# Stage 1 of a three-block kernel: small PSUM transposes in quarters of one bank, up-projections on the general ring

## The chip, the cores and the metric

One NeuronCore of one Trainium2 chip runs the whole program. The metric is device time in microseconds (us), the median of repeated runs; lower is better. The engines are PE (TensorE: matmuls and transposes), ACT (ScalarE), DVE (VectorE), POOL (GpSimd) and SP, which here only issues DMAs. Each engine takes its own instructions strictly in order, and waits at an instruction until the semaphores that it names have been raised. PSUM, where PE writes its results, has eight banks of 128 partitions by 512 fp32 values.

## The reference

Three blocks follow each other on a batch of 8 sequences of 576 tokens and 512 features; only the first, with the token half of the second, matters for the change.

```python
a = exp(phi - max(phi, axis=seq)); a = a / sum(a, axis=seq)      # phi: 8, 8 heads, 576, 32
k_m, v_m = einsum('bhsm,bhsd->bhmd', a, k), einsum('bhsm,bhsd->bhmd', a, v)
attn = softmax(q @ k_m.T / sqrt(64)); x = attn @ v_m             # 576 x 64 per head
u = x + (relu(x.T @ w_tok1) @ w_tok2).T                          # mixes tokens
x = u + relu(u @ w_ch1) @ w_ch2                                  # mixes channels: up, then down
# then a mixture of 4 causal attention experts, two for each token
```

## The kernel before

Most matrix products are made of three: each fp32 operand is split in a high part (fp32r) and the rest, and hi·hi, hi·lo and lo·hi are summed in PSUM (`mm3`, whose matmuls all have line 250). Scores, transposes and the sums over the sequence run in plain fp32 on PE.

Stage 1 goes over 16 units: one batch row and four heads each. A unit has three parts. `front` takes the maximum of phi over the sequence (DVE `top`, then PE transposes it, `top_t`; DVE reduces, `top_c`; PE transposes the result back over all partitions, `top_b`; DVE subtracts, `e_sub`; ACT takes exp), sums k and v with it on PE (`kv_mm`, tile g), scales k (DVE `k_scale`, tile kr; ACT, tile ks), transposes k (`k_t`, copied out by ACT `k_c`, tile kmT) and transposes q (`q_t`: two full banks of four transposes each, and a small one of the last 32 rows, copied to qTb). `rows` makes the scores, their softmax and the transposes of the attention (`to_rows`, a full bank; `to_rows_end`, a small one read by ACT `hi5` and DVE `lo5`). `mix` does the token product and writes u (`u_a`, `u_b`). At the end `ahead` reloads the first 512 columns of u and computes the first four up-projections of the next stage (`up`, 12 matmuls each, whose results go through ACT `up_hi` and DVE `up_lo`). Stage 2 goes on with the down-projections, tiles o0 to o3.

The order on every engine in stage 1 is not written out by hand. A planner (`Plan`) holds each step with an assumed length, its inputs and the PSUM ring that it takes a place of; `search` shuffles the steps' ranks 400 times, keeps the order that ends first by its own reckoning, and so writes all five queues. A change in the rings therefore reorders the whole stage. `filled` puts idle matmuls (`spin`, 128 by 128 zeros in bf16) in the gaps that the planner sees on PE in its first 70 us. The waits themselves are set later by the framework, from what each instruction reads and writes.

In stage 1 the eight banks of PSUM are: ring t with two banks (all transposes, large and small, one to a bank), ring g with four (everything else), and two banks h of a pool `ppw` of their own, that hold the first up-projections and the target of the spins. `ppw` lives on into stage 2.

Of the kernel before, what the change touches and what calls it, by code (L numbers as in the profile page):

```python
# [10 lines left out]
F32 = mybir.dt.float32  # L11
# [4 lines left out]
AF = mybir.ActivationFunctionType  # L16
OP = mybir.AluOpType
AX = mybir.AxisListType
PSUM = bass.MemoryType.PSUM
# [190 lines left out]
def fused_kernel(ctx: ExitStack, tc, q, k, v, phi, w_tok1, w_tok2, w_ch1, w_ch2,  # L210
# [3 lines left out]
    M = phi.shape[3]  # L214
# [7 lines left out]
    SH = S // 2  # L222
# [4 lines left out]
    PE, ACT, DVE, POOL, SP = nc.tensor, nc.scalar, nc.vector, nc.gpsimd, nc.sync  # L227
# [62 lines left out]
    wch_ctx, b0_ctx, stg_ctx, sw_ctx = ExitStack(), ExitStack(), ExitStack(), ExitStack()  # L290
    wbm = wch_ctx.enter_context(tc.tile_pool(name="wbm", bufs=1, reuse_waits="tile"))
    wu = b0_ctx.enter_context(tc.tile_pool(name="wu", bufs=1, reuse_waits="tile", side="right"))
    ppw = sw_ctx.enter_context(tc.tile_pool(name="ppw", bufs=1, space=PSUM, reuse_waits="tile", side="right"))
    w1h, w1l, w2h, w2l = {}, {}, {}, {}

    def ch_weights(pool, spool, fc, wd, nb, ws=(0, 1)):
# [21 lines left out]
    with ExitStack() as sa:  # L318
# [24 lines left out]
        for i in range(NB2):  # L343
# [2 lines left out]
        units = [(b, g) for b in range(B) for g in range(2)]  # L346
        NU, NR = len(units), 2
        NB = S // 32
        plan = Plan(pools=dict(t=2, g=4, h=2, cst=5, cy=2, cm=2),
                    ahead=dict(PE=0, ACT=90, DVE=70, POOL=-60),  # L350
                    hop=dict(PE=230, ACT=60, DVE=120, POOL=120, SP=1900), stay=2000)
        add, free = plan.add, plan.free
        MM, TR = 133.4, 109

        def psum(name, shape=(128, 512)):
            return pp.tile(list(shape), F32, name=name, bufs=4 if name == "g" else 2)

        def loads(n):
            b, g = units[n]
# [25 lines left out]
        def front(n):  # L385
# [7 lines left out]
                DVE.tensor_reduce(mx[:], ph[:].rearrange("p h j m -> p h m j"), axis=AX.X, op=OP.max)  # L393

            def top_t():
                st["p"] = psum("t", (128, 128))
                PE.transpose(st["p"][:], st["mx"][:].rearrange("p h m -> p (h m)"), ident[:])

            def top_c():
                st["mc"] = wk_.tile([128, 1], F32, name="pmc", bufs=2)  # L400
                DVE.tensor_reduce(st["mc"][:], st["p"][:], axis=AX.X, op=OP.max)

            def top_b():
                st["p"] = psum("t", (128, 128))
                PE.transpose(st["p"][:], st["mc"][:].to_broadcast([128, 128]), ident[:])

            def e_sub():
                e = st["e"] = wk_.tile([128, 4, 5, M], F32, name="ea", bufs=2)
                bc = st["p"][:].rearrange("p (h m) -> p h m", h=4)[:, :, None, :].to_broadcast([128, 4, 5, M])
                DVE.tensor_sub(e[:], ph[:], bc)  # L410

            def e_exp():
# [51 lines left out]
                POOL.tensor_mul(st[y][:], src[:, None, :].to_broadcast([128, 4, 64]), vmask[:])  # L464

            def k_t():
                st["p"] = psum("t", (128, 128))
                PE.transpose(st["p"][:], st["ks"][:].rearrange("p a d -> p (a d)"), ident[:])

            def k_c():  # L470
                st["km"] = wk_.tile([128, 128], F32, name="kmT", bufs=2)
                ACT.activation(st["km"][:], st["p"][:], AF.Copy)

            def q_t(i):
                if i < 2:
                    p = st["q", i] = psum("t")
                    for x in range(4):
                        PE.transpose(p[:, 128 * x:128 * x + 128],  # L478
                                     qn_[:, 2 * i + x // 2, 2 * (x % 2):2 * (x % 2) + 2, :].rearrange("p j d -> p (j d)"),
                                     ident[:])  # L480
                    return
                st["q", 2] = psum("t", (128, 4, 32))
                for h in range(4):
                    PE.transpose(st["q", 2][:, h, :], qe_[:, h, :], ident[0:32, 0:32])

            def q_c(i):
                if i < 2:
                    ACT.activation(qT[:, 2 * i:2 * i + 2, 0:256].rearrange("k h (p j) -> k h j p", j=2),
                                   st["q", i][:].rearrange("k (h j p) -> k h j p", h=2, j=2), AF.Copy)
                else:  # L490
                    ACT.activation(qT[:, :, 256:SH], st["q", 2][:], AF.Copy)

            add("DVE", 1320, top, reads=[kph], writes=["mx"])
            a = add("PE", TR, top_t, kind="f", reads=["mx"], writes=[(n, "pt")], take="t")
            c = add("DVE", 270, top_c, reads=[(n, "pt")], writes=[(n, "mc")])
            free(a, c)
            a = add("PE", TR, top_b, kind="f", reads=[(n, "mc")], writes=[(n, "pb")], take="t")
            c = add("DVE", 820, e_sub, reads=[(n, "pb"), kph], writes=[("e", n % 2)])
            free(a, c)
            add("ACT", 735, e_exp, reads=[("e", n % 2)], writes=[("e", n % 2)])  # L500
# [6 lines left out]
            c = add("ACT", 360, k_mul, reads=[(n, "g"), (n, "r")], writes=["ks"])  # L507
            d = add("ACT", 315, v_scale, reads=[(n, "g"), (n, "r")], writes=["vm"])
            free(g_, c, d)
            a = add("PE", TR, k_t, kind="f", reads=["ks"], writes=[(n, "pk")], take="t")  # L510
            c = add("ACT", 260, k_c, reads=[(n, "pk")], writes=[kkm])
            free(a, c)
            add("POOL", 560, v_split, reads=["vm"], writes=["vh", "vl"], port=True)
            add("POOL", 760, lambda: v_mask("vh", "Vh"), reads=["vh"], writes=[("Vh", n % 3)], port=True)
            add("POOL", 760, lambda: v_mask("vl", "Vl"), reads=["vl"], writes=[("Vl", n % 3)], port=True)
            for i in range(3):
                a = add("PE", (440, 440, 400)[i], lambda i=i: q_t(i), kind="f", reads=["qn"], writes=[(n, "q", i)], take="t")
                c = add("ACT", (625, 625, 275)[i], lambda i=i: q_c(i), reads=[(n, "q", i)], writes=[(*kqT, i)])
                free(a, c)

        def rows(n):
# [44 lines left out]
                    PE.transpose(p[:, 128 * j:128 * j + 128], st["a"][:, 128 * j:128 * j + 128], ident[:])  # L566

            def to_rows_end():
                st["p5"] = psum("t", (128, 128))
                PE.transpose(st["p5"][0:ST, :], st["a"][:, SM:S], ident[:])  # L570

            def hi4():
# [30 lines left out]
            h4 = add("ACT", 600, hi4, reads=[(n, "p4")], writes=["hi4"])  # L603
            l4 = add("DVE", 690, lo4, reads=[(n, "p4"), "hi4"], writes=["lo4"])
            free(a4, h4, l4)
            a5 = add("PE", TR, to_rows_end, kind="f", reads=[("a", n % 2)], writes=[(n, "p5")], take="t")
            h5 = add("ACT", 265, hi5, reads=[(n, "p5"), "hi4"], writes=["hi5"])
            l5 = add("DVE", 285, lo5, reads=[(n, "p5"), "hi5"], writes=["lo5"])
            free(a5, h5, l5)
# [94 lines left out]
        def ahead():  # L704
            def opened():
                stg_ctx.close()
                ld_ctx.close()
                st["b0"] = b0_ctx.enter_context(tc.tile_pool(name="b0", bufs=1, reuse_waits="tile", side="right"))
                load_u(0, st["b0"])
                uh[0] = st["b0"].tile([128, KD, 512], F32R, name="uh")  # L710
                ul[0] = st["b0"].tile([128, KD, 512], F32R, name="ul")

            def s_hi(kd):
                ACT.activation(uh[0][:, kd, :], ub[0][:, kd, :], AF.Copy)

            def s_lo(kd):
                DVE.tensor_sub(ul[0][:, kd, :], ub[0][:, kd, :], f(uh[0][:, kd, :]))

            def up(fc):
                st[fc] = ppw.tile([128, 512], F32, name="h", bufs=2)  # L720
                mm3(st[fc][:], [((w1h[fc][:, kd, :], w1l[fc][:, kd, :]), (uh[0][:, kd, :], ul[0][:, kd, :]))
                                for kd in range(KD)])

            def up_hi(fc):
                hs[0, fc] = [st["b0"].tile([128, 512], F32R, name=x, bufs=4) for x in ("hh", "hl")]
                ACT.activation(hs[0, fc][0][:], st[fc][:], AF.Relu)

            def up_lo(fc):
                DVE.scalar_tensor_tensor(hs[0, fc][1][:], st[fc][:], 0.0, f(hs[0, fc][0][:]), op0=OP.max, op1=OP.subtract)

            st = rest
            add("SP", (600, 4300), opened, reads=[("ud", 0), ("ud", 1)], writes=["ub"], after=[U[NU - 1]["score"], *convs])
            for kd in range(KD):
                add("ACT", 600, lambda kd=kd: s_hi(kd), reads=["ub"], writes=[("bh", kd)])
                add("DVE", 700, lambda kd=kd: s_lo(kd), reads=["ub", ("bh", kd)], writes=[("bl", kd)], port=True)
            for fc in range(NA):
                a = add("PE", 12 * 227, lambda fc=fc: up(fc), reads=[(x, kd) for x in ("bh", "bl") for kd in range(KD)] + [("w1", fc)],
                        writes=[("up", fc)], take="h")
                c = add("ACT", 600, lambda fc=fc: up_hi(fc), reads=[("up", fc)], writes=[("fh", fc)])
                d = add("DVE", 690, lambda fc=fc: up_lo(fc), reads=[("up", fc), ("fh", fc)], writes=[("fl", fc)])  # L740
                free(a, c, d)
# [112 lines left out]
        ahead()  # L854
        ET = mybir.EngineType
        with tc.manual_schedule(engines={ET.PE, ET.Activation, ET.DVE, ET.Pool, ET.SP}):
            idle = ppw.tile([128, 512], F32, name="h", bufs=2)

            def spin():
                PE.matmul(idle[:, 0:128], lhsT=still[:, 0:128], rhs=still[:], start=True, stop=True)  # L860

            for fn in plan.filled(70000, 0.6, 56, spin):
                fn()
# [35 lines left out]
    with ExitStack() as sb:  # L899
# [3 lines left out]
        wkx = wkx_ctx.enter_context(tc.tile_pool(name="wkx", bufs=1, reuse_waits="tile"))  # L903
        stg = stg_ctx.enter_context(tc.tile_pool(name="stgb", bufs=2, reuse_waits="tile"))
        pp = sb.enter_context(tc.tile_pool(name="ppb", bufs=1, space=PSUM, reuse_waits="tile"))
        def split_pool(n):
            return wkx if n % 2 else wk_

# [756 lines left out]
```

## Time and profile before

| | |
|---|---|
| median of 3 runs | 1188.08 us (1187.22 to 1189.03) |
| profiled execution | 1188.45 us, of which the trace's span is 1186.7 us |
| PE busy | 1162.8 us (98% of the span) |
| DVE, ACT, POOL busy | 785.3, 594.2, 406.6 us |
| granted TensorE clock, mean | 0.997 |

Busy time of PE contains the spins, and a matmul's end is modelled, so that a busy PE may still be short of its peak. The first matmul of stage 2's down-projections stands at 241.7 us: stage 1 is the first fifth of the span.

### The profile page before, as it was taken

The page shows a single profiled execution, that of the slowest core. Times are in us where ns is not written, and L with a number is a line of the kernel's source. Part 1 is how long each engine was busy: PE and PEld are TensorE (multiplying, and loading weights), DVE is VectorE, ACT ScalarE, POOL GpSimd, SP SyncE. Part 2 cuts the span into 40 slices and gives each one's busy share as a digit, 9 for nine tenths or more (in the row PEclk, how much of TensorE's full clock was granted, in tenths as well). Part 3 has the DMA queues.
Part 4 walks back from the last instruction along what each step waited for, and adds up shares of the span by engine and source line. Part 5 has one row for each costly group of instructions (what it writes and reads, how often), then busy time and mean ns, then how long its engine had stood idle before and what let it go on. Part 6 is the DMA issues. An engine that isn't in the chain of part 4 may idle for free.

```text
span 1186.7 us, 23501 instructions
## 1 busy us (share of the span) xinstructions
PE 1162.8 (98%) x8668; PEld 1055.3 (89%) x8668; DVE 785.3 (66%) x1942; ACT 594.2 (50%) x1533; POOL 406.6 (34%) x575
## 2 busy tenths in 40 slices
PE   7999999999999999999999999999999999999998
PEld 6778878888888999898998889999999999999986
DVE  6889997386755656647563624877766777677763
ACT  3566666443322222313221214777676767676774
POOL 3667566100001010101000445637272727373331
PEclk9999999999999999999999999999999999999999
DMA  9888884262030312203020444313232323222423
GB/s 274 224 256 254 264 263 162 73 218 66 17 107 1 107 36 72 81 27 107 1 99 1 146 134 121 103 46 104 66 114 65 122 84 109 79 83 62 160 88 107
DMA packets 125075, 133.54 MB, mean 113 GB/s; under 512 B 35232, under 2 KB 94624, under 8 KB 124960
## 3 DMA queue, kind: packets, MB, share of 16 engines
q1 hardware_dynamic: 124960, 132.03, 37.1%
q8 instruction: 69, 1.13, 0.4%
q14 instruction: 46, 0.38, 0.1%
HBM read 89.01 MB, written 31.46 MB: 102 GB/s over the span
## 4 chain that ended last, share of the span: by engine, by line
PE 84%; DVE 8%; POOL 2%; issue 2%; ACT 2%; DMA 1%; SPq 0%; ACTq 0%; DVEq 0%; POOLq 0%
PE g L250 23%; PE o L250 21%; PE h L250 20%; PE y L1437 4%; PE s L1328 3%; PE t L1392 3%; PE s L1350 1%; PE g L662 1%; PE g L668 1%; PE g L671 1%; PE g L669 1%; POOL a L1373 1%; PE t L478 1%; PE t L250 1%; DVE pmx L393 1%
## 5 line engine op out<-in xcount | busy, mean ns | idle before, releaser
L978 POOL TENSOR_TENSOR tl<-ub,th 128x512 fp32r<-128x512 f32 x12 | 18.2, 1539 | 358.4 <-ACT th L977 358.4
L250 PE MATMUL o<-hl,w2h 128*128 128x512 f32 x360 | 141.0, 392 | 0.0
L250 PE MATMUL o<-hh,w2l 128*128 128x512 f32 x360 | 140.6, 391 | 0.0
L250 PE MATMUL o<-hh,w2h 128*128 128x512 f32 x360 | 135.5, 391 | 0.0
L1373 POOL TENSOR_TENSOR a<-a,cf 128x128 f32<-128x128 f32 (+3 forms) x128 | 88.3, 724 | 70.6 <-DVE cf L1365 63.6
L930 ACT ACTIVATE hh<-m 128x256 fp32r<-128x256 f32 x120 | 48.9, 417 | 126.0 <-DVE m L1001 65.9
L1317 DVE CUSTOM_DVE_ANT_0 ssb<-s,cmask 128x128 f32<-128x128 f32 (+2 forms) x144 | 68.8, 483 | 31.1 <-PE s L1328 18.2
L250 PE MATMUL h<-uh,w1l 128*128 128x512 f32 (+2 forms) x248 | 82.6, 335 | 0.0
L250 PE MATMUL h<-uh,w1h 128*128 128x512 f32 (+2 forms) x248 | 82.6, 334 | 0.0
L250 PE MATMUL h<-ul,w1h 128*128 128x512 f32 (+2 forms) x248 | 82.4, 335 | 0.0
L1330 ACT ACTIVATE a<-ssb,nb 128x128 f32<-128x128 f32 (+3 forms) x128 | 71.4, 558 | 21.3 <-DVE nb L1317 17.7
L250 PEld LDWEIGHTS o<-hh,w2l 128*128 128x128 f32 x360 | 67.6, 188 | 14.4
L250 PEld LDWEIGHTS o<-hl,w2h 128*128 128x128 f32 x360 | 67.6, 188 | 12.6 <-DVE hl L923 0.5
L250 PEld LDWEIGHTS o<-hh,w2h 128*128 128x128 f32 x360 | 67.6, 188 | 12.3
L931 DVE SCALAR_TENSOR_TENSOR hl<-m,hh 128x256 fp32r<-128x256 f32 x120 | 58.7, 497 | 17.8 <-ACT hh L930 15.1
L1229 POOL TENSOR_TENSOR xl<-p,xh 128x288 fp32r<-128x288 f32 x60 | 47.6, 813 | 52.0 <-ACT xh L1228 49.9
L250 PE MATMUL g<-xh,qkh 128*128 128x288 f32 x232 | 65.3, 301 | 0.0
L250 PE MATMUL g<-xh,qkl 128*128 128x288 f32 x232 | 64.0, 296 | 0.0
L994 ACT ACTIVATE m<-h 128x256 f32<-128x256 f32 x30 | 11.6, 385 | 101.5 <-PE h L250 101.5
L257 DVE TENSOR_TENSOR Bl<-t,Bh 128x512 fp32r<-128x512 f32 (+1 forms) x80 | 50.4, 633 | 14.6 <-ACT Bh L254 13.2
L996 DVE TENSOR_TENSOR m<-m,h 128x256 f32<-128x256 f32 x30 | 12.6, 421 | 71.5 <-PE h L250 70.5
L250 PEld LDWEIGHTS h<-uh,w1h 128*128 128x128 f32 x248 | 46.8, 189 | 6.9
(331 smaller groups left out, 3800.1 us busy)
## 6 DMA issues: line engine op xcount, KB each, us to landing
cst<-in_moe_w_ch_dram SPq DMA_DIRECT2D x24, 512.0 KB, 5.7
u_d<-u SPq DMA_DIRECT2D x32, 288.0 KB, 3.2
ub<-u_d SPq DMA_DIRECT2D x9, 1024.0 KB, 5.0
u<-u_d SPq DMA_DIRECT2D x16, 576.0 KB, 4.0
p<-x_d SPq DMA_DIRECT2D x15, 576.0 KB, 4.1
kv<-in_k_dram SPq DMA_DIRECT2D x16, 512.0 KB, 6.2
kv<-in_v_dram SPq DMA_DIRECT2D x16, 512.0 KB, 6.1
qn<-in_q_dram SPq DMA_DIRECT2D x16, 512.0 KB, 5.4
```

Source lines behind the costliest of these rows:

```text
L250: PE.matmul(ps, lhsT=a, rhs=b, start=start and i == 0, stop=stop and i == len(seq) - 1)
L257: DVE.tensor_sub(lo, src, f(hi))
L930: ACT.activation(hh, c, AF.Relu)
L931: DVE.scalar_tensor_tensor(hl, c, 0.0, f(hh), op0=OP.max, op1=OP.subtract)
L978: (DVE if i in (1, 2) else POOL).tensor_sub(tl[n][:, i], q_, f(th[n][:, i]))
L1229: POOL.tensor_sub(xl[b][:, c, ss], x_, f(xh[b][:, c, ss]))
L1317: DVE.tensor_tensor_reduce(out=out, in0=p, in1=mask, scale=-scale, scalar=least, op0=OP.add, op1=OP.min, accum_out=acc)
L1328: PE.matmul(p[:, 0:W], lhsT=q_[n][:, 128 * c:128 * c + 128], rhs=kk[n][:, 0:W], start=(i == 0), stop=(i == 1))
L1330: ACT.activation(a[:, aoff[c]:aoff[c] + W], s_[:, 0:W], AF.Exp, scale=-1.0, bias=nb[:, 0:1], accum_out=sm[:, c:c + 1])
L1373: POOL.tensor_mul(x_, x_, cf[:, c:c + 1].to_broadcast([128, W]))
L1392: PE.transpose(p[:, 128 * kc:128 * kc + 128], a[:, o + 128 * kc:o + 128 * kc + 128], ident[:])
L1437: PE.matmul(p[:, lo:w], lhsT=v_[:, kc, 0, :], rhs=x, start=(i == 0), stop=(i == len(ops) - 1))
```

## The change

The small transposes (`top_t`, `top_b`, `k_t`, the last part of `q_t`, `to_rows_end`) leave ring t. They share one tile `small` of one bank, in turn in its first three quarters of 128 columns; the planner knows them as a ring q with three places. The spins write the fourth quarter, which nobody reads. The bank count becomes t 2, q 1, g 5. The up-projections of `ahead` take places of ring g, and `ppw` is opened only in stage 2.

```diff
-    ppw = sw_ctx.enter_context(tc.tile_pool(name="ppw", bufs=1, space=PSUM, reuse_waits="tile", side="right"))
...
-        plan = Plan(pools=dict(t=2, g=4, h=2, cst=5, cy=2, cm=2),
+        plan = Plan(pools=dict(t=2, g=5, q=3, cst=5, cy=2, cm=2),
...
+        small, turned = pp.tile([128, 4, 128], F32, name="q"), [0]
+
+        def psum(name):
+            return pp.tile([128, 512], F32, name=name, bufs=dict(t=2, g=5)[name])
+
+        def part():
+            turned[0] += 1
+            return small[:, turned[0] % 3, :]
...
             def top_t():
-                st["p"] = psum("t", (128, 128))
-                PE.transpose(st["p"][:], st["mx"][:].rearrange("p h m -> p (h m)"), ident[:])
+                st["p"] = part()
+                PE.transpose(st["p"], st["mx"][:].rearrange("p h m -> p (h m)"), ident[:])
...
-            a = add("PE", TR, k_t, kind="f", reads=["ks"], writes=[(n, "pk")], take="t")
+            a = add("PE", TR, k_t, kind="f", reads=["ks"], writes=[(n, "pk")], take="q")
...
             def up(fc):
-                st[fc] = ppw.tile([128, 512], F32, name="h", bufs=2)
+                st[fc] = psum("g")
...
-                        writes=[("up", fc)], take="h")
+                        writes=[("up", fc)], take="g")
...
-            idle = ppw.tile([128, 512], F32, name="h", bufs=2)
-
             def spin():
-                PE.matmul(idle[:, 0:128], lhsT=still[:, 0:128], rhs=still[:], start=True, stop=True)
+                PE.matmul(small[:, 3, :], lhsT=still[:, 0:128], rhs=still[:], start=True, stop=True)
...
+        ppw = sw_ctx.enter_context(tc.tile_pool(name="ppw", bufs=1, space=PSUM, reuse_waits="tile", side="right"))
```

Three places show how the queues move. The first is the head of SP's queue, the loads that the first units wait for. In the kernel before, phb_106 is the phi of unit 0 and phb_107 that of unit 1; kv_112 belongs to unit 0.

```order
L370 DMA kv_112<-in_k_dram 128x4x256
L372 DMA kv_112<-in_k_dram 64x4x64
L370 DMA kv_112<-in_v_dram 128x4x256
L372 DMA kv_112<-in_v_dram 64x4x64
L364 DMA phb_106<-in_phi_dram 128x4x128
L366 DMA phb_106<-in_phi_dram 64x4x32
L376 DMA qn<-in_q_dram 128x4x256
L378 DMA qe<-in_q_dram 32x4x128
L364 DMA phb_107<-in_phi_dram 128x4x128
L366 DMA phb_107<-in_phi_dram 64x4x32
```

In the changed kernel unit 0's phi is phb_103, unit 1's is phb_104:

```order
L375 DMA kv_109<-in_k_dram 128x4x256
L377 DMA kv_109<-in_k_dram 64x4x64
L369 DMA phb_104<-in_phi_dram 128x4x128
L371 DMA phb_104<-in_phi_dram 64x4x32
L375 DMA kv_109<-in_v_dram 128x4x256
L377 DMA kv_109<-in_v_dram 64x4x64
L381 DMA qn<-in_q_dram 128x4x256
L383 DMA qe<-in_q_dram 32x4x128
L369 DMA phb_103<-in_phi_dram 128x4x128
L371 DMA phb_103<-in_phi_dram 64x4x32
```

The two phi loads have changed places: that of unit 0 is now the ninth and tenth instruction, behind q, where unit 1's stood.

The second place is PE's queue where unit 3's k is transposed (`k_t`, tile ks) and `u_a` of unit 0 (tiles aT, Vh, Vl) follows; behind the names stand the engines whose semaphores an instruction waits for. Before:

```order
L622 MATMUL g<-t1l,ahi 128x256
L468 MATMUL t<-ident,ks 128x128 [waits DVE_49,Activation_49]
L662 MATMUL g<-aT,Vh 128x288 [waits PE_49]
L662 MATMUL g<-aT,Vh 128x288 [waits Activation_49]
L662 MATMUL g<-aT,Vl 128x288 x2
```

And in the changed kernel, where six spins stand between the two (one row of weights and one of matmul each):

```order
L410 MATMUL q<-ident,pmc 128x128
L863 LDWEIGHTS still
L863 MATMUL q<-still 128x128
L473 MATMUL q<-ident,ks 128x128 [waits Activation_49]
L863 LDWEIGHTS still
L863 MATMUL q<-still 128x128 [waits Activation_49]
...
L667 MATMUL g<-aT,Vh 128x288 [waits PE_49] x2
```

The first of the six spins has got a wait for ACT; what it waits for is ACT's copy of the transposed k (L477, kmT). That copy in turn waits for a DVE instruction, the `e_sub` (L415) that reads another quarter. Of the 302 spins of the changed kernel 23 wait for ACT or DVE; of the 310 before none does.

The third place is PE's queue at the end of stage 1: the last matmuls of the last up-projection, and the first down-projection (o, from the hidden values hh and hl). Before, the up-projection of the fifth group of 128 hidden channels (w1h_3327) stands between:

```order
L668 MATMUL g<-t2h,hh 128x288
L669 MATMUL g<-t2l,hh 128x288
L671 MATMUL g<-t2h,hl 128x288 x2
L250 MATMUL h<-uh,w1h_3327 128x512 [waits DVE_49]
L250 MATMUL h<-ul,w1h_3327 128x512
L250 MATMUL h<-uh,w1l_3328 128x512
...
L250 MATMUL o_3993<-hh,w2h_1918 128x512 [waits Activation_49]
L250 MATMUL o_3993<-hl,w2h_1918 128x512
```

In the changed kernel:

```order
L676 MATMUL g<-t2h,hl 128x288 x2
L250 MATMUL g<-uh,w1h_1587 128x512 [waits Activation_49]
L250 MATMUL g<-ul,w1h_1587 128x512
L250 MATMUL g<-uh,w1l_1588 128x512
...
L250 MATMUL o_3905<-hh,w2h_1784 128x512 [waits Activation_49]
L250 MATMUL o_3905<-hl,w2h_1784 128x512 [waits DVE_49]
```

The down-projection now follows the last of the four early up-projections at once, and reads the hidden values of that very one; the fifth up-projection comes later.

## Rows read from the trace of the kernel before

**Rows 1.** Busy time by engine, granted clock and DMA in three stretches.

```profile
core 0: us, PE busy (x) PEld busy (x) DVE busy (x) ACT busy (x) POOL busy (x), PEclk, DMA share, GB/s
50.00:72.00 22.00, 21.92 (x266) 18.81 (x264) 15.43 (x30) 13.10 (x32) 12.72 (x20) 1.00 0.82 243
72.00:242.00 170.00, 166.09 (x1681) 140.48 (x1681) 135.77 (x248) 103.75 (x240) 94.22 (x111) 1.00 0.69 212
242.00:1186.00 944.00, 935.16 (x6077) 860.96 (x6075) 596.75 (x1592) 456.35 (x1220) 274.33 (x410) 1.00 0.28 84
```

**Rows 2.** Waits of PE from 50 to 242 us: total, times, longest.

```profile
PE t L570 <- DVE alo L578: 1.1, 1, 1.1
PE t L468 <- ACT qTb L488: 0.7, 1, 0.7
PE t L484 <- DVE ea L410: 0.7, 1, 0.7
```

**Rows 3.** Timeline of the start: start, us, engine, line, output<-input, count, idle time before.

```profile
9.43 1.23 DVE L393 TENSOR_REDUCE pmx<-phb 128x128 f32<-128x640 f32 x1 [6.04 <-DMA phb<-in_phi_dram]
...
10.81 0.30 PE L397 MATMUL t<-ident,pmx 128*128 128x128 f32 x1 [2.50 <-DVE pmx L393]
...
11.15 0.29 DVE L401 TENSOR_REDUCE pmc<-t 128x1 f32<-128x128 f32 x1 [0.49 <-PE t L397]
...
12.61 1.27 DVE L393 TENSOR_REDUCE pmx<-phb 128x128 f32<-128x640 f32 x1 [1.16 <-DMA phb<-in_phi_dram]
...
14.39 0.82 DVE L410 TENSOR_TENSOR ea<-phb,t 128x640 f32<-128x640 f32 x1 [0.51 <-PE t L405]
...
16.17 0.82 DVE L410 TENSOR_TENSOR ea<-phb,t 128x640 f32<-128x640 f32 x1
...
16.45 1.30 PE L428 MATMUL g<-kv,ea 128*32 128x128 f32 x40
```

**Rows 4.** Timeline, units 0 to 2: kr, k_t, a q_t that waits, e_sub, kv_mm.

```profile
19.88 0.15 DVE L444 TENSOR_SCALAR kr<-g 128x1 f32<-128x1 f32 x1
...
21.02 0.33 PE L468 MATMUL t<-ident,ks 128*128 128x128 f32 x1 [1.46 <-ACT ks L449]
...
29.32 1.12 PE L478 MATMUL t<-ident,qn 128*128 128x128 f32 x4 [2.78 <-ACT qTb L488]
...
32.07 0.81 DVE L410 TENSOR_TENSOR ea<-phb,t 128x640 f32<-128x640 f32 x1
...
34.32 1.30 PE L428 MATMUL g<-kv,ea 128*32 128x128 f32 x40
```

**Rows 5.** What one costs: a run of 24 spins; e_sub and k_c, ns min/median/max.

```profile
18.04 1.34 PEld L860 LDWEIGHTS <-still 128*128 128x128 bf16 x24
...
L410 DVE TENSOR_TENSOR ea<-phb,t x16: 760/811/833, 14.4 to 181.8; 128x640 f32<-128x640 f32 x16
...
L472 ACT ACTIVATE kmT<-t x16: 251/275/308, 21.6 to 202.4; 128x128 f32<-128x128 f32 x16
```

**Rows 6.** Timeline of PE: unit 3's k_t and the u_a behind it.

```profile
50.74 0.27 PE L468 MATMUL t<-ident,ks 128*128 128x128 f32 x1
50.94 0.40 PE L662 MATMUL g<-aT,Vh 64*128 64x288 f32 x2
```

**Rows 7.** Timeline of PE: three fp32r matmuls behind fp32 transposes.

```profile
64.57 0.39 PE L621 MATMUL g<-t1h,ahi 128*128 128x256 f32 x1
...
64.80 0.28 PE L622 MATMUL g<-t1l,ahi 128*128 128x256 f32 x1
...
64.92 0.28 PE L621 MATMUL g<-t1h,ahi 128*128 128x256 f32 x1
```

**Rows 8.** Timeline, end of stage 1: last matmul of an up-projection, up_hi, up_lo.

```profile
237.79 0.39 PE L250 MATMUL h<-uh,w1l 128*128 128x512 f32 x1
...
238.22 0.60 ACT L726 ACTIVATE hh<-h 128x512 fp32r<-128x512 f32 x1 [2.35 <-PE h L250]
...
238.85 0.69 DVE L729 SCALAR_TENSOR_TENSOR hl<-h,hh 128x512 fp32r<-128x512 f32 x1 [5.64 <-ACT hh L726]
```

More of the change, by code (lines that the diff above doesn't have):

```diff
@@ L353, in fused_kernel @@
         MM, TR = 133.4, 109
-        def psum(name, shape=(128, 512)):
-            return pp.tile(list(shape), F32, name=name, bufs=4 if name == "g" else 2)
+        small, turned = pp.tile([128, 4, 128], F32, name="q"), [0]
[4 more added lines that the diff above has]
+            return small[:, turned[0] % 3, :]
         def loads(n):
@@ L395, in top_t @@
             def top_t():
-                st["p"] = psum("t", (128, 128))
-                PE.transpose(st["p"][:], st["mx"][:].rearrange("p h m -> p (h m)"), ident[:])
+                st["p"] = part()
+                PE.transpose(st["p"], st["mx"][:].rearrange("p h m -> p (h m)"), ident[:])
             def top_c():
                 st["mc"] = wk_.tile([128, 1], F32, name="pmc", bufs=2)
-                DVE.tensor_reduce(st["mc"][:], st["p"][:], axis=AX.X, op=OP.max)
+                DVE.tensor_reduce(st["mc"][:], st["p"], axis=AX.X, op=OP.max)
             def top_b():
-                st["p"] = psum("t", (128, 128))
-                PE.transpose(st["p"][:], st["mc"][:].to_broadcast([128, 128]), ident[:])
+                st["p"] = part()
+                PE.transpose(st["p"], st["mc"][:].to_broadcast([128, 128]), ident[:])
             def e_sub():
                 e = st["e"] = wk_.tile([128, 4, 5, M], F32, name="ea", bufs=2)
-                bc = st["p"][:].rearrange("p (h m) -> p h m", h=4)[:, :, None, :].to_broadcast([128, 4, 5, M])
+                bc = st["p"].rearrange("p (h m) -> p h m", h=4)[:, :, None, :].to_broadcast([128, 4, 5, M])
                 DVE.tensor_sub(e[:], ph[:], bc)
@@ L466, in k_t @@
             def k_t():
-                st["p"] = psum("t", (128, 128))
-                PE.transpose(st["p"][:], st["ks"][:].rearrange("p a d -> p (a d)"), ident[:])
+                st["p"] = part()
+                PE.transpose(st["p"], st["ks"][:].rearrange("p a d -> p (a d)"), ident[:])
             def k_c():
                 st["km"] = wk_.tile([128, 128], F32, name="kmT", bufs=2)
-                ACT.activation(st["km"][:], st["p"][:], AF.Copy)
+                ACT.activation(st["km"][:], st["p"], AF.Copy)
             def q_t(i):
@@ L481, in q_t @@
                     return
-                st["q", 2] = psum("t", (128, 4, 32))
+                st["q", 2] = part().rearrange("p (h k) -> p h k", h=4)
                 for h in range(4):
@@ L490, in q_c @@
                 else:
-                    ACT.activation(qT[:, :, 256:SH], st["q", 2][:], AF.Copy)
+                    ACT.activation(qT[:, :, 256:SH], st["q", 2], AF.Copy)
             add("DVE", 1320, top, reads=[kph], writes=["mx"])
-            a = add("PE", TR, top_t, kind="f", reads=["mx"], writes=[(n, "pt")], take="t")
+            a = add("PE", TR, top_t, kind="f", reads=["mx"], writes=[(n, "pt")], take="q")
             c = add("DVE", 270, top_c, reads=[(n, "pt")], writes=[(n, "mc")])
             free(a, c)
-            a = add("PE", TR, top_b, kind="f", reads=[(n, "mc")], writes=[(n, "pb")], take="t")
+            a = add("PE", TR, top_b, kind="f", reads=[(n, "mc")], writes=[(n, "pb")], take="q")
             c = add("DVE", 820, e_sub, reads=[(n, "pb"), kph], writes=[("e", n % 2)])
@@ L516, in front @@
             for i in range(3):
-                a = add("PE", (440, 440, 400)[i], lambda i=i: q_t(i), kind="f", reads=["qn"], writes=[(n, "q", i)], take="t")
+                a = add("PE", (440, 440, 400)[i], lambda i=i: q_t(i), kind="f", reads=["qn"], writes=[(n, "q", i)], take="tq"[i == 2])
                 c = add("ACT", (625, 625, 275)[i], lambda i=i: q_c(i), reads=[(n, "q", i)], writes=[(*kqT, i)])
@@ L568, in to_rows_end @@
             def to_rows_end():
-                st["p5"] = psum("t", (128, 128))
+                st["p5"] = part()
                 PE.transpose(st["p5"][0:ST, :], st["a"][:, SM:S], ident[:])
@@ L605, in rows @@
             free(a4, h4, l4)
-            a5 = add("PE", TR, to_rows_end, kind="f", reads=[("a", n % 2)], writes=[(n, "p5")], take="t")
+            a5 = add("PE", TR, to_rows_end, kind="f", reads=[("a", n % 2)], writes=[(n, "p5")], take="q")
             h5 = add("ACT", 265, hi5, reads=[(n, "p5"), "hi4"], writes=["hi5"])
```

## The prediction

> **What bounds the kernel now.** I read the table by stretches first. From 242 us on PE is busy for 935.16 of 944 us, and the change touches nothing there, so only stage 1 can move the time. In stage 1 the table tells two phases apart. From 50 to 72 us PE is busy for 21.92 of 22 us and from 72 to 242 us for 166.09 of 170 us, while DVE has 135.77 of 170: PE sets the pace, and it has 170 - 166.09 = 3.9 us of idle time left [rows 1]. The matmuls of the stage are the same before and after, so in this phase a microsecond that PE stands still is a microsecond of the end. Before 50 us the first units come in through a chain of loads, DVE and PE, and PE fills its gaps with spins; what counts there is when the first units' work gets to PE. Next I read PE's waits: the ones on a bank of ring t that a reader still holds are short, 1.1 + 0.7 + 0.7 = 2.5 us in three places [rows 2]. That is nearly all that more room for transposes can give back after 50 us. Then the timeline of the start and of the end of the stage, for the steps below, and the new order for what stands where.
>
> **What the framework makes of the quarters.** The planner counts three independent places in ring q. The order of the changed kernel shows something else: 23 spins, which write a quarter that nobody reads, wait for ACT or DVE, and none did before. The waits go by the bank, not by the quarter. PE may write a quarter only when the readers of all other quarters that stand earlier in the program are done, and a reader waits for the earlier writes and for the other engine's earlier reader too. The Trainium skill ("PSUM — Partial Sum Buffer", "PSUM bank collisions raise a hardware error") says that two engines may not touch the same bank and the same 32 partitions at once, whatever the columns, and that it is the program that must keep them apart. By that rule quarters cut by columns are one place, not three; a guard by address would take the new waits below out of the sum and leave a gain of about 1.7 us. No trace here shows such a collision.
>
> **The change part by part.**
>
> (a) *The start.* Unit 0's phi stands where unit 1's stood in SP's queue, with the same bytes ahead of it, so its `top` starts at 12.61 us, not at 9.43 [rows 3]. From there: 12.61 + 1.27 = 13.88; the transpose and its reduction start 0.03 and 0.37 later (10.81 to 11.15 is 0.34) and end 0.29 after that, at 14.54; then DVE has unit 1's `top` (1.27, to 15.8), and unit 0's `e_sub` also has to wait for the transpose of that one, in another quarter (0.03 + 0.34): 16.2 us in place of 14.39. It hides part of the loss, since before it stood behind q's transposes. `kv_mm` of unit 0 follows 19 spins that wait for this `e_sub`; a spin takes 1.34/24 = 0.056 us [rows 5], so 16.2 + 0.81 + 0.05 + 19 x 0.056 = 18.1 against 16.45. On DVE the way from `e_sub` to unit 0's kr is what it was from unit 1's (16.17 to 19.88, 3.7 us [rows 3, 4]), with about 0.9 more for two steps moved in: 16.2 + 3.7 + 0.9 = 20.8, 0.9 late. Then `k_t`: 13 spins in front of it wait for unit 1's `e_sub`, which DVE ends some 1.6 us after kr, at 22.4; with 13 x 0.056 = 0.7 `k_t` comes at 23.2 against 21.02, 2.2 late, and the scores, behind 5 spins that now follow k's copy, 2.5 late. Unit 1 regains the 2.78 us that a q transpose waited for ring t [rows 4], because small tiles no longer take its banks; it loses 19 spins behind a reader (1.1), 6 more (0.3) and k's copy that is now ahead of unit 2's `e_sub` (0.28). So `kv_mm` of unit 2 should stand about 2.5 - 2.8 + 1.7 = 1.4 us later than 34.32. I take **+1.4**; bounds 0 (if it is regained before 50 us) and 2.5.
>
> (b) *Spins between 45 and 72 us.* PE has no idle time there to hide them. Unit 3's `k_t` was followed by `u_a` 0.20 us later [rows 6]. Now the spin between them waits for k's copy, and the copy for `e_sub`, which waits for `k_t`: 0.34 + 0.81 + 0.05 + 0.28 + 0.05 = 1.5, less 0.12 that `k_t` itself occupies, is 1.4 us of PE standing still [rows 3, 5]. Behind the next `to_rows_end` a spin waits for `hi5`, which on ACT is behind such a copy again: 0.34 + 0.81 + 0.05 + 0.28 + 0.27 + 0.05 = 1.8, less 0.9 for the six `u_b` in between and the transpose, is 0.8. Three more places wait for one reader, which I put at 0.35 each. Sum **+3.2**; lower bound 0 (the readers done long before PE comes), upper bound five times 1.4 = 7.
>
> (c) *Small transposes after 72 us.* The 2.5 us of waits on ring t go [rows 2]. In the new order I find seven places where a transpose stands closer behind a reader of another quarter than that reader's chain is long (a copy of 0.28 behind an `e_sub` of 0.81, and the like), 0.3 to 1.1 us each, 3.5 together. Net **+1.0**; bounds -2.5 and 7 x 1.4 - 2.5 = 7.3.
>
> (d) *Grouping on PE.* With five banks g the planner puts more of one kind together: leaving the spins out, PE's queue changes between fp32 and fp32r work 139 times before and 95 times now, 22 round trips fewer. Behind fp32 transposes the first fp32r matmul takes 64.80 - 64.57 = 0.23 to the next start, the second 0.12 [rows 7]: 0.11 a trip. **-2.4**; bounds 0 and twice that, -4.8, if the way back costs as much. Eight spins fewer are 0.4 us of time in which PE has nothing else to do, so nothing.
>
> (e) *The end of the stage.* The first down-projection needs the hidden values of the last up-projection. From the start of an up's last matmul (237.79) to the end of `up_hi` it is 238.82 - 237.79 = 1.03, to the end of `up_lo` 239.54 - 237.79 = 1.75 [rows 8]. PE would go on after 0.23; it waits 0.8, issues one matmul (0.23), and waits 0.5 for the second. Before, a whole up-projection (12 x 0.23 = 2.8) covered this. **+1.3**; lower bound 0 if DVE and ACT run ahead there, upper bound 1.8 if they are late by what is queued ahead.
>
> Sum: 1.4 + 3.2 + 1.0 - 2.4 + 1.3 = **+4.5 us**. The profiled execution took 1188.45, 0.4 above the median and inside the spread of the three runs (1.8), so I put the sum on the median: 1188.08 + 4.5 = 1192.6.
>
> **Rivals.** 0.2% of the time, 2.4 us, is about what a measurement of this kernel can tell from no change.
>
> *Faster: the fifth bank g pays.* PE's 3.9 us of idle time goes, the grouping gives 2.4, and the bank's waits fall where the operands of the next matmul are not there anyway, so (a), (b) and the new part of (c) are nothing; (e) stays. 1188.1 - 3.9 - 2.4 + 1.3 = 1183. For it speaks that the small tiles did block ring t, once for 2.78 us; against it that PE in 50 to 72 us has no idle time to hide a wait. It decides at unit 2's `kv_mm`: if that starts before 34.3, it is this case or the next.
>
> *No change: the start is regained and the readers are early.* (a) 0.5, (b) and (c) together 0.5, (d) -2.4, (e) 1.3: 1188. For it speaks that DVE and ACT have slack after 72 us (80% and 61% busy), so that readers are mostly prompt.
>
> *Much slower: the shared bank couples ACT and DVE.* Some sixteen of the 96 readers of the bank now wait for a reader on the other engine that they have nothing to do with; at up to 0.81 each that is 13 us on in-order queues, and if half of it reaches PE, 6.5 more: 1199. Against it: the reader ahead mostly stands a microsecond earlier.
>
> **How the numbers follow.** Forecast (1190.5 to 1197) 0.50, much slower 0.16, no change 0.20, faster 0.14. So slower by over 0.2% is 0.66, within 0.2% is 0.20, faster is 0.14. The predicted time is the forecast's sum, 1192.6. Low end 1186.5, which takes in the case of no change, since the lower bounds of (a) to (c) are all open; high end 1200, which takes in the coupling. Both ends together leave out about 0.18.
>
> **What would show it.** (a) unit 2's `kv_mm` between 35 and 37 us. (b) PE's busy time from 50 to 75 us below the 99% of before, with waits of spins on ACT kmT, ACT ahi and DVE of 0.3 to 1.4 us. (c) waits of small transposes (tile q) on DVE and ACT after 72 us of 3 to 4 us in sum, and none on ring t. (d) fewer long intervals at the changes of kind. (e) a gap of 1 to 1.5 us on PE just before the first o matmul, which should stand at about 246 us in place of 241.7. If that first o matmul stands at 242 or earlier, the prediction is wrong, and the place where PE was ahead of the 34.32 or of the 72 us mark tells which of (a) to (c) failed.

## The result and the profile after

The changed kernel takes 1198.26 us (median of 4 runs, 1196.51 to 1198.74), the kernel before 1188.55 in the same comparison: a ratio of 1.0079, 95% interval 1.0061 to 1.0096, 9.7 us by the medians. The direction was foreseen and the time lies inside the stated range, but the forecast's sum was +4.5 us: half of what came. The band that the prediction gave to its own forecast, 1190.5 to 1197, ends below 1198.26. The profiled execution took 1198.26 us. Its page starts:

```profile
span 1196.5 us, 23456 instructions
PE 1164.2 (97%) x8660; PEld 1055.1 (88%) x8660; DVE 786.0 (66%) x1942; ACT 595.0 (50%) x1533; POOL 407.4 (34%) x575
```

PE works as long as before (1164.2 against 1162.8 us), and the span is 9.8 us longer: the time went into standing still. The table by stretches tells where (its columns are those of [rows 1]):

```profile
30.00:40.00 10.00, 6.38 (x86) 4.42 (x82) 8.03 (x16) 3.85 (x9) 7.87 (x11) 0.68 0.77 213
...
50.00:72.00 22.00, 19.82 (x277) 16.08 (x278) 15.96 (x32) 10.88 (x26) 16.38 (x23) 1.00 0.73 210
72.00:242.00 170.00, 164.69 (x1700) 140.99 (x1700) 139.53 (x249) 106.74 (x243) 95.26 (x113) 1.00 0.69 209
```

From 50 to 72 us PE now idles 2.18 us, where it idled 0.08 [rows 1]. From 72 to 242 us it idles 5.31 against 3.91: hardly more. From 30 to 40 us it is busy for 6.38 us at a mean clock of 0.68 of full speed, and DVE, which had been the busy engine of the start, for 8.03. Before, the same stretch shows 8.67, 0.88 and 9.36:

```profile
30.00:40.00 10.00, 8.67 (x142) 7.51 (x141) 9.36 (x17) 4.64 (x9) 7.36 (x10) 0.88 1.13 257
```

The first o matmul has moved from 241.57 (the 241.7 given ahead of the prediction is 0.1 too late) to 246.33, but that is not the whole delay: before, the fifth up-projection (12 matmuls) was behind PE at that point, and now it is still to come. A place with the same work behind it in both kernels is the first matmul h from th and sh in stage 2. In the timeline of PE, of before:

```profile
335.47 0.28 PE L250 MATMUL h<-th,sh 128*128 128x256 f32 x1
```

and of the changed kernel:

```profile
343.67 0.28 PE L250 MATMUL h<-th,sh 128*128 128x256 f32 x1
```

The delay out of stage 1 is 8.20 us. Some 0.3 to 0.6 us are added by small shifts later, and about 1 at the very end, where DVE's last copy waits for an earlier store of its buffer, 4.43 us where it waited 2.57.

To place the 8.2 us, I gave each shape of matmul the time from its start to the next that it takes in the kernel before (spins left out), added these up along PE's queue in each kernel, and compared when the same sum was reached. Since the kinds stand in another order, a single value is good to 1 us or so; the last column is the landmark above, or the same measure there.

```
us later than the kernel before, when before stands at   50    72   160   240   335
changed kernel                                          +5.5  +8.7  +7.0  +7.7  +8.2
changed kernel without spins                            +2.8  +3.0  +1.1  +1.8  +2.3
```

All of the 8.2 us is there at 72 us, 5.5 of it at 50. What goes wrong in the start can be read from PE's timeline, from unit 2's `top_t` (L402) to its `kv_mm` (L433):

```profile
30.70 0.30 PE L402 MATMUL q<-ident,pmx 128*128 128x128 f32 x1 [0.57 <-DVE pmx L398]
32.83 1.55 PE L863 MATMUL q<-still 128*128 128x128 bf16 x19 [1.84 <-DVE pmc L406]
34.17 0.42 PE L410 MATMUL q<-ident,pmc 128*128 128x128 f32 x1
...
34.50 0.42 PE L473 MATMUL q<-ident,ks 128*128 128x128 f32 x1
36.14 0.80 PE L863 MATMUL q<-still 128*128 128x128 bf16 x6 [1.22 <-DVE ea L415]
36.87 1.21 PE L536 MATMUL g<-qTb,kmT 64*32 64x288 f32 x16
38.01 1.14 PE L863 MATMUL q<-still 128*128 128x128 bf16 x9
39.09 1.91 PE L433 MATMUL g<-kv,ea 128*32 128x128 f32 x40
```

Both stops of PE stand in front of a run of spins. Nineteen matmuls that compute nothing wait 1.84 us for a DVE reduction, because they write the bank that it reads and the framework guards the bank as one place; six more wait 1.22 us for unit 2's `e_sub`. Behind the first run stand `top_b`, which needs that reduction itself, and unit 1's `k_t`; behind the second stand unit 1's scores, which don't need the `e_sub`. DVE's side of the same place:

```profile
31.11 0.75 DVE L556 TENSOR_REDUCE ssm<-ssb 128x18 f32<-128x576 f32 x1 [0.55 <-ACT ssb L552]
...
32.51 0.27 DVE L406 TENSOR_REDUCE pmc<-q 128x1 f32<-128x128 f32 x1
32.70 1.26 DVE L768 TENSOR_SCALAR cm<-cm 128x512 f32<-128x512 f32 x1
35.26 0.82 DVE L415 TENSOR_TENSOR ea<-phb,q 128x640 f32<-128x640 f32 x1 [1.30 <-ACT kmT L477]
```

The reduction is late because on DVE it stands behind unit 0's softmax sums, and `e_sub` waits 1.30 us for ACT's copy of another quarter, which waits for `k_t`, which stands behind the spins. PE's waits from 50 to 242 us complete the picture (total, times, longest):

```profile
PE q L863 <- DVE pmc L406: 1.5, 2, 1.2
PE q L863 <- ACT kmT L477: 1.2, 1, 1.2
PE q L402 <- ACT kmT L477: 0.8, 1, 0.8
PE q L402 <- DVE ahi L589: 0.7, 1, 0.7
PE q L863 <- ACT ahi L586: 0.6, 1, 0.6
PE q L575 <- DVE ea L415: 0.6, 1, 0.6
PE q L473 <- DVE ea L415: 0.6, 1, 0.6
PE q L489 <- DVE ahi L589: 0.4, 1, 0.4
PE q L863 <- DVE ahi L589: 0.3, 1, 0.3
PE q L575 <- ACT kmT L477: 0.2, 1, 0.2
PE q L473 <- DVE ahi L589: 0.2, 1, 0.2
```

The waits on ring t [rows 2] are gone. The small transposes (every line but L863) wait 3.5 us in sum for readers of other quarters, and the spins 3.6.

### The profile page after: what moved, and what is told of

Its sections match the earlier page's. It is cut to its first block, busy times and chain, and to the rows that moved or that the text cites. A ratio compares the mean times of both kernels' runs of the same rounds, so it can differ in the third digit from the quotient of the medians.

```text
span 1196.5 us, 23456 instructions
## 1 busy us (share of the span) xinstructions
PE 1164.2 (97%) x8660; PEld 1055.1 (88%) x8660; DVE 786.0 (66%) x1942; ACT 595.0 (50%) x1533; POOL 407.4 (34%) x575
## 4 chain that ended last, share of the span: by engine, by line
PE 85%; DVE 7%; issue 2%; DMA 2%; POOL 2%; ACT 1%; SPq 1%; DVEq 0%; ACTq 0%; POOLq 0%
PE g L250 23%; PE o L250 20%; PE h L250 19%; PE y L1441 4%; PE s L1332 3%; PE t L1396 3%; PE s L1354 1%; PE g L673 1%; PE g L667 1%; PE g L676 1%; PE g L674 1%; PE q L863 1%; PE g L433 1%; POOL a L1377 1%; PE t L483 1%
## 5 line engine op out<-in xcount | busy, mean ns | idle before, releaser
L250 PE MATMUL h<-uh,w1l 128*128 128x256 f32 (+2 forms) x232 | 76.6, 332 | 0.0
L250 PE MATMUL h<-uh,w1h 128*128 128x256 f32 (+2 forms) x232 | 76.1, 330 | 0.0
L250 PE MATMUL h<-ul,w1h 128*128 128x256 f32 (+2 forms) x232 | 76.1, 331 | 0.0
L254 ACT ACTIVATE Bh<-t 128x512 fp32r<-128x512 f32 (+1 forms) x80 | 44.0, 552 | 14.8 <-PE t L1396 5.7
```

The source lines that it names most:

```text
L250: PE.matmul(ps, lhsT=a, rhs=b, start=start and i == 0, stop=stop and i == len(seq) - 1)
L254: ACT.activation(hi, src, AF.Copy)
```

## The experiments

My theory was now: the spins that write the shared bank are what costs, and the new order itself little (**spin theory**). The rival: the planner's new order costs, above all the late phi of unit 0 (**order theory**).

**1. Only the spins' bank.** With the spins moved out of the shared bank a ninth bank would be needed, so this pair has four banks g and one that is free, and the planner counts with four. Stage 1 stands in the same order in both, though not in that of the changed kernel.

```diff
-        plan = Plan(pools=dict(t=2, g=5, q=3, cst=5, cy=2, cm=2),
+        plan = Plan(pools=dict(t=2, g=4, q=3, cst=5, cy=2, cm=2),
...
+        idle = pp.tile([128, 512], F32, name="idle")
...
-            return pp.tile([128, 512], F32, name=name, bufs=dict(t=2, g=5)[name])
+            return pp.tile([128, 512], F32, name=name, bufs=dict(t=2, g=4)[name])
```

> The changed kernel with four banks g in place of five (in the planner and in PSUM) and one bank that nothing uses, so that the next run can move the spins there with the same order of stage 1. Spin theory (spins that write the shared bank stand behind readers of its other quarters, and PE behind the spins): 1194 to 1200 us, as slow as the changed kernel, with over 8 us of spins waiting for DVE or ACT before 72 us. Rival, order theory (the planner's new order is what costs, above all unit 0's phi behind q): its order loads phi of both units third and fourth and so is not late, 1188 to 1192.

The second of the pair has this edit too:

```diff
-                PE.matmul(small[:, 3, :], lhsT=still[:, 0:128], rhs=still[:], start=True, stop=True)
+                PE.matmul(idle[:, 0:128], lhsT=still[:, 0:128], rhs=still[:], start=True, stop=True)
```

> The same, with the spins writing the unused bank: the order of stage 1 is that of the run before on every engine, and only the spins' bank differs. Spin theory: 4 to 7 us faster than with the shared bank, unit 2's kv_mm 3 to 5 us earlier, no spin that waits for DVE or ACT. Order theory: within 1.5 us of the run before.

Measured: 1194.44 us with the shared bank (1.0042 of before, 1.0025 to 1.0059), 1190.34 with a bank of their own (1.0012, 1.0002 to 1.0023): 4.1 us apart. The groups of the spins say why; what PE waited for in front of them, shared:

```profile
L864 PE MATMUL q<-still x305: 216/219/314, 1.1 to 78.4; 128*128 128x128 bf16 x153
...
  DVE ea L416: 5.1, 4
  ACT ahi L587: 2.1, 2
  ACT kmT L478: 1.4, 4
  DVE pmc L407: 1.3, 3
  DVE still L237: 1.1, 1
```

and in their own bank:

```profile
L864 PE MATMUL idle<-still x305: 216/219/314, 1.1 to 71.4; 128*128 128x128 bf16 x153
...
  DVE still L237: 1.1, 1
```

The same 305 spins wait 9.9 us for readers in one kernel and not at all in the other (the 1.1 us is their operand's memset). In stage 2 the first 256-wide matmul h from uh and w1h stands at 340.99 shared and at 334.25 with a bank of their own, 6.7 us apart; with the own bank some of that is lost again near the end of the kernel, where one matmul waits 2.6 us for ACT's copy of an output (0.4 at most in the other). The spin theory holds, in stage 1 at the upper end of what it expected. Unit 2's `kv_mm` came 3.2 us earlier (31.31 against 34.48). Shared was less slow than the changed kernel, at the lower end of the expected 1194.

**2. No spins at all.** The spin is left out of the changed kernel, and in the same way of the kernel before; the order of each is untouched:

```diff
             def spin():
-                PE.matmul(small[:, 3, :], lhsT=still[:, 0:128], rhs=still[:], start=True, stop=True)
+                pass
```

> The changed kernel without any spin (idle matmuls only, the computation is whole), its order untouched. Spin theory: the 8 us of waits of spins before 50 us and 3.6 us behind go, some of it is lost again since PE idles more and its clock is granted at half more often: 2 to 5 us faster than the changed kernel, 1193 to 1196. Order theory: no faster than the changed kernel, 1198 or more, since what the waits hid behind stays late.

> The kernel before without any spin, as the pair of the last run: what the spins are worth where they wait for nobody. Both theories: 0 to 4 us slower than before (1188 to 1192), with the clock at half in more stretches of the first 50 us. Spin theory: it is at most 5 us ahead of the changed kernel without spins, where with spins the two are 9.7 apart; order theory: 8 to 11 us ahead of it.

Measured: 1191.33 without spins in the changed kernel (1.0019 of before, 1.0010 to 1.0029), 6.9 us faster than with them, more than the spin theory expected. The kernel before without spins takes 1189.59 (1.0010, 0.9999 to 1.0020). The two are 1.7 us apart where with spins they are 9.7, and by the landmark 1.5 (337.77 and 336.29). This is the strongest result: about three quarters of the loss go with the spins, in an order that is exactly that of the changed kernel. The place shown above, without them:

```profile
31.67 0.48 PE L402 MATMUL q<-ident,pmx 128*128 128x128 f32 x1
32.72 0.32 PE L410 MATMUL q<-ident,pmc 128*128 128x128 f32 x1 [0.56 <-DVE pmc L406]
33.01 0.33 PE L473 MATMUL q<-ident,ks 128*128 128x128 f32 x1
33.71 0.72 PE L536 MATMUL g<-qTb,kmT 64*32 64x288 f32 x16 [0.37 <-ACT kmT L477]
35.39 2.19 PE L433 MATMUL g<-kv,ea 128*32 128x128 f32 x40 [0.96 <-ACT ea L418]
```

`top_t` is a microsecond later than with spins, and `kv_mm` of unit 2 3.7 us earlier. Two more rows of this run, unit 0's `k_t` and the reduction that held the nineteen spins:

```profile
24.29 0.45 PE L473 MATMUL q<-ident,ks 128*128 128x128 f32 x1 [2.17 <-DVE ea L415]
...
32.39 0.27 DVE L406 TENSOR_REDUCE pmc<-q 128x1 f32<-128x128 f32 x1
```

The reduction starts at 32.39 here and at 32.51 with spins, so the 1.84 us in front of the nineteen spins are not their price at this place: `top_b` behind them has to wait for it in any case. Their price is that they run after the wait: `top_b` starts at 34.17 in place of 32.72, 1.45 us later. The six spins hold the scores for an `e_sub` that the scores don't need; the scores start at 36.87 in place of 33.71, which is 1.7 us more. The row at 24.29 shows the shared bank at work without any spin: `k_t` waits 2.17 us for unit 1's `e_sub` in another quarter. Before, it stood at 21.02 and waited for its own operand [rows 4].

**3. The late phi of unit 0.**

```diff
...
-            for fn in plan.filled(70000, 0.6, 56, spin):
+            fns = plan.filled(70000, 0.6, 56, spin)
+            a, b = [fns.index(x) for x in phis[0:2]]
+            fns[a], fns[b] = fns[b], fns[a]
+            for fn in fns:
```

> The changed kernel with one thing put back: the loads of unit 0's and unit 1's phi change places in the planner's finished order, so that unit 0's stands third and fourth in SP's queue. All other steps keep their place. Phi theory (the late phi of unit 0 starts the chain that ends at unit 2's kv_mm): 2 to 4 us faster than the changed kernel, unit 2's kv_mm at 36 to 37 in place of 39.1. Spin theory: unit 0's kv_mm comes up to 2 us earlier, but the spins in front of unit 1's k_t and unit 2's k_t wait for the same readers, so at most 1.5 us faster.

Measured: 1197.57 (1.0067, 1.0051 to 1.0083), 0.7 faster than the changed kernel, inside the intervals. Unit 2's `kv_mm` stands at 39.39, no earlier than 39.09, where the phi theory had 36 to 37, and unit 0's came no earlier either: 18.67 against 17.93. PE's timeline shows why an early `top` helps nobody:

```profile
10.77 0.60 PE L489 MATMUL q<-ident,qe 32*128 32x32 f32 x4 [2.74 <-DMA qe<-in_q_dram]
11.31 1.97 PE L483 MATMUL t<-ident,qn 128*128 128x128 f32 x8
13.07 1.45 PE L863 MATMUL q<-still 128*128 128x128 bf16 x15
14.36 0.28 PE L402 MATMUL q<-ident,pmx 128*128 128x128 f32 x1
```

The transposes of q stand in front of unit 0's `top_t` in PE's queue, and wait for their own load. In this execution the granted clock was 0.50 from 11 to 14 us, behind the idle time before them, and eight of them took 1.76 us to the next start in place of 0.93, so unit 0's times are not a clean pair. But the changed kernel itself bounds what the phi can give back: unit 0's `top_t` waits 0.23 us there for its reduction of phi, and DVE's next steps stand behind it.

```profile
13.57 0.33 PE L402 MATMUL q<-ident,pmx 128*128 128x128 f32 x1 [0.23 <-DVE pmx L398]
```

The late phi is no cause of this loss; the order theory loses its main part.

**4. The other half of the change alone.** Up-projections in ring g with five banks, spins in a bank of their own, small transposes in ring t as before.

```diff
-        plan = Plan(pools=dict(t=2, g=4, h=2, cst=5, cy=2, cm=2),
+        plan = Plan(pools=dict(t=2, g=5, cst=5, cy=2, cm=2),
...
-                st[fc] = ppw.tile([128, 512], F32, name="h", bufs=2)
+                st[fc] = psum("g")
...
-            idle = ppw.tile([128, 512], F32, name="h", bufs=2)
+            idle = pp.tile([128, 512], F32, name="idle")
...
```

> The other part of the change alone: the up-projections go to ring g, which has five banks, the spins keep a bank of their own, and the small transposes stay in ring t with its two banks. If the fifth bank and the new place of the up-projections are worth little or nothing by themselves: 1187 to 1190. If they pay: a down-projection before 240 us and 1183 to 1186. If the missing cover at the end of the stage and a new order cost: 1191 or more.

Measured: 1189.86 (1.0006, 0.9997 to 1.0016), no difference that can be told; the landmark is 0.4 us later than in before. The fifth bank, the missing cover at the end of the stage and this kernel's own order come to about nothing together.

**5. A planner that knows the truth.** The changed kernel without spins, ring q with one place:

```diff
-        plan = Plan(pools=dict(t=2, g=5, q=3, cst=5, cy=2, cm=2),
+        plan = Plan(pools=dict(t=2, g=5, q=1, cst=5, cy=2, cm=2),
```

> The changed kernel without spins, with the planner told that ring q has one place (the tile and its quarters stay as they are). The run without spins still waited 4.7 us for tile q behind 50 us. If the planner's belief in three places causes these waits: under 1.5 us of them, and 2 to 3 us faster than the changed kernel without spins, 1188 to 1189.5. If the order of the small transposes is not what is left: within 1 us of it, 1190.5 to 1192, or slower, since one place makes the planner hold transposes back.

Measured: 1191.80 (1.0027, 1.0016 to 1.0038), the same as with three places (1191.33). The waits for tile q behind 50 us fell from 4.7 to 2.5 us, 0.6 of it a load, and others took their place (1.4 on DVE's `at`, 0.9 on a load of q). The first of the two expectations, a gain, is wrong: with 2.2 us less of these waits the time was the same. The order of the start is another one too, so what the waits are worth by themselves stays open.

**6. Room without sharing.** Three banks t, five banks g, no shared bank, and no spins, since no bank is left for them; on top of the edit of experiment 4 and without its idle bank:

```diff
+        plan = Plan(pools=dict(t=3, g=5, cst=5, cy=2, cm=2),
...
+            return pp.tile(list(shape), F32, name=name, bufs=5 if name == "g" else 3)
...
             def spin():
+                pass
```

> No shared bank at all: ring t with three banks for all transposes, ring g with five and the up-projections in it, and no spins. What the change wanted (more room for transposes and for everything else), without the shared bank. If room in PSUM is worth something here: 1184 to 1187. If it isn't, since before had only 2.5 us of waits on ring t behind 50 us, and a planner's order without spins costs about 1 us: 1187 to 1191.

Measured: 1185.80 (0.9974, 0.9964 to 0.9983), faster than both kernels, by 3.1 us over before.

**7. The luck of the search.** The same kernels with another seed:

```diff
-        rng = random.Random(1)
+        rng = random.Random(2)
```

> The kernel before with another seed of the planner's search (2 in place of 1), so another order of stage 1 with the same banks. It says how much of a difference between two kernels can be the luck of the search. If the draws lie close: 1187 to 1191. If luck is as large as the effects told of here: more than 4 us away from before, on either side.

> The changed kernel with the same other seed; 19 of its spins wait for DVE or ACT in place of 23. Spin theory: again 4 to 10 us slower than the kernel before with this seed. Luck theory (the first seed drew a bad order for the changed kernel): within 3 us of it.

> The run before without its spins, the order untouched. Spin theory: 3 to 7 us faster than with them. Luck theory: within 1.5 us, since spins cost little in another order.

> Three banks t, five banks g, no shared bank and no spins, with the other seed. If the gain of the first seed (1185.8 against 1188.9) comes from the room in PSUM: 1184 to 1188, and faster than the kernel before with this seed. If it was a lucky draw: 1188 to 1192.

Measured: before 1188.54 (0.9995, 0.9986 to 1.0004), changed 1194.21 (1.0040, 1.0026 to 1.0055), changed without spins 1189.99 (1.0011, 1.0001 to 1.0021), three banks t 1188.20 (0.9995, 0.9986 to 1.0004). The signs hold and the sizes don't: the change costs 5.7 us with this seed (9.7 with the first), of which the spins are 4.2 (6.9). So some 4 us of the first seed's loss hang on the order that was drawn. The gain of experiment 6 shrinks to 0.3 us, which cannot be told from nothing: two draws don't show that room without sharing is worth anything, though neither was slower than before.

## Why the prediction was half right

**What the framework makes of the quarters: right, and the main cause.** The waits go by the bank. The Trainium skill ("PSUM — Partial Sum Buffer", "PSUM bank collisions raise a hardware error") asks for guards by bank and quadrant rather than by address; the trace agrees in that quarters of columns were guarded as one place, and the pair of experiment 1 gives the price of the guard where idle work shares the bank, 4.1 us. No run here left the guard out. The gain of 1.7 us that the prediction saw for a guard by address does not come out of its terms: without the new waits in (a), 1.7, in (b), 3.2, and in (c), 3.5, the sum of 4.5 would be -3.9.

**(a) The start: mis-sized, +1.4 foreseen and 4.8 measured.** Unit 2's `kv_mm` stands at 39.09, not at 34.32 [rows 4], and outside the term's bounds (0 to 2.5). Much of the working was right: unit 0's `kv_mm` at 17.93 (18.1 foreseen), `k_t` at 23.82 (23.2), and unit 2's `top_t` is only 0.47 late. Two steps failed. The first is that unit 1 "regains the 2.78 us": `top_t` shows it, but the reduction behind it on DVE does not. Before:

```profile
28.78 0.75 DVE L551 TENSOR_REDUCE ssm<-ssb 128x18 f32<-128x576 f32 x1 [0.32 <-ACT ssb L547]
...
30.68 0.29 DVE L401 TENSOR_REDUCE pmc<-t 128x1 f32<-128x128 f32 x1 [0.64 <-PE t L397]
```

Now it starts at 32.51, 1.8 us later, because unit 0's softmax sums, which began at 28.78 and now begin at 31.11, stand ahead of it on DVE. The working asked what is queued behind a wait, but not what is queued ahead of the reader. The second is "it loses 19 spins behind a reader (1.1), 6 more (0.3) and k's copy", 1.7 in sum. From the reduction to `kv_mm` it took 34.32 - 30.68 = 3.64 us before and takes 39.09 - 32.51 = 6.58 now, 2.9 more. Against the run without spins the nineteen cost 1.45, and the six with k's copy 1.7, where 0.6 was foreseen: they wait 1.22 us for an `e_sub` that itself waits 1.30 for the copy. It also left out the clock. PE had stood still, and the trace shows the granted clock at 0.50 (1.2 of 2.4 GHz) from 34 to 40 us; there the scores take 1.15 us to the next start in place of 0.65, and the nine spins behind them, which the sum doesn't have, 1.07 in place of 9 x 0.056 = 0.50. The start of the chain was misplaced too: phi's late load, with which the working began, costs next to nothing (experiment 3).

**(b) Spins from 45 to 72 us: right, as far as the measure goes.** +3.2 foreseen; the measure of lag, good to 1 us, grows from 5.5 at 50 us to 8.7 at 72, and the spins wait 2.7 us for readers from 45 to 72 us. Of the places named, the spin behind unit 3's `k_t` waited 1.22 for ACT's kmT (1.4 foreseen), the one behind `to_rows_end` 0.58 for ahi (0.8), and one on `top_c`'s reduction 0.30 (0.35).

**(c) Small transposes after 72 us: right in size.** 3.5 us of such waits were foreseen from 72 us on; 3.5 are read in the waits from 50 to 242 us, and none is left on ring t. PE's idle time from 72 to 242 us grew by 1.4 us (+1.0 foreseen). Spins wait another 1.5 us there, which the sum has nowhere. In experiment 5 such waits gave way to others when they were taken out: as a sum of prices the term may be less than it looks.

**(d) and (e).** The first o matmul came 0.85 us and the second 0.50 us later than PE's spacing of 0.23 asks, 1.35 together (+1.3 foreseen):

```profile
245.25 0.40 PE L250 MATMUL g<-uh,w1l 128*128 128x512 f32 x1
246.33 0.50 PE L250 MATMUL o<-hh,w2h 128*128 128x512 f32 x1 [0.69 <-ACT hh L731]
247.06 0.50 PE L250 MATMUL o<-hl,w2h 128*128 128x512 f32 x1 [0.22 <-DVE hl L734]
```

The grouping (-2.4 foreseen) is only inferred: from 72 us to the landmark the lag fell by 0.5 although idle time grew by 1.4 and by (e)'s 1.35, which leaves about -3, with an uncertainty of 1 us. No run tried it by itself.

So the sum failed in one term: the 1.4 of (a) should have been 4.8. With it the sum is 7.9, against 8.2 at the landmark; that they are so close leans on (d), which is read from the same lag. The last 1.5 us came behind 242 us, where the prediction had said that the change touches nothing. That the time lies inside the range is luck: only the high end, 1200, which was set for the rival "much slower", takes it in.

**The rivals.** The test that the prediction named for the faster case, and for no change, was unit 2's `kv_mm` before 34.3; it came at 39.1, and both are out. The rival "much slower" had the right size (1199) by another mechanism: ACT's and DVE's readers that wait for each other. They do (1.30 us in the rows above), and without spins the bank still holds needed work back (`k_t`'s 2.17 us in experiment 2): the lag without spins is 3.0 us at 72. Against before without spins 1.5 us are left at the landmark, and 1.7 at the end. What the coupling costs by itself, and how much of it the new order and the grouping give back, no run separates. What made most of the loss was work on PE that nobody needed, standing in front of work that was needed.

## What to carry to other kernels

Work that fills idle time must be able to start at any moment: give it a target that no reader ever holds, or leave it out. Ask of a bank cut into parts by which unit the waits are set, and tell a planner that number of places; and price a wait by what stands ahead of the reader on its own queue, not by the reader's length. Before idle work is blamed for a wait in front of it, ask whether the work behind it needs the same reader anyway. Where a search writes the order, compare a change over more than one seed before a few microseconds are believed.

## What the runs showed of the hardware

The 310 spins of the kernel before are worth 1.1 us (1189.59 without them, ratio 1.0010 with an interval that touches 0.9999). The clock does fall without them; of the kernel before without spins (columns as in [rows 1]):

```profile
30.00:40.00 10.00, 6.67 (x69) 3.87 (x67) 9.58 (x18) 4.66 (x10) 7.36 (x10) 0.66 1.11 282
40.00:50.00 10.00, 8.56 (x88) 7.08 (x89) 6.00 (x12) 4.81 (x11) 7.31 (x11) 0.66 0.57 144
```

In these stretches the mean was 0.88 and 1.00 with spins. Up to 30 us the column reads 1.00, but unit 0's `kv_mm` tells of a PE at about half speed, 2.36 us in place of 1.30 [rows 3]:

```profile
16.27 2.36 PE L428 MATMUL g<-kv,ea 128*32 128x128 f32 x40
```

So the lengths of the matmuls should be read beside that column. Why the slower PE costs so little is only argued: from 30 to 40 us DVE is busy for 9.58 of 10 us and PE for 6.67, so PE has slack there; from 40 to 50 us DVE is busy for 6.00 alone. I had taken the spins as given, and had not expected that leaving them out would be nearly free.
